# Expert 0's first half on the first 512 tokens, as two parts of 256 tokens, the first started 24 stops earlier in the attention loop

## The chip, the cores and the metric

The kernel runs on one core of a Trainium2 chip. Its engines work side by side, each on its own queue in its own order: TensorE (PE for its matmuls, PEld for its weight loads), VectorE (DVE), ScalarE (ACT), GpSimd (POOL) and SyncE (SP, which issues transfers). The metric is the device time of one execution in microseconds (us); lower is better. Three executions of the kernel before took 1479.65 to 1479.95 us, median 1479.87.

## What is computed

Three layers in a row, all in float32: windowed attention with sink keys, a mixture of 8 experts whose gates come from a Sinkhorn iteration, and a mixture of 8 experts that sends each token to one of them.

```python
# attention: B=2, H=8 heads, S=768 tokens, D=64; 4 sink keys, window 128
scores = where(keep, scale * q @ k.T, -1e9)
a = softmax(scores); x = (a @ v)           # -> 1536 tokens x 512
# first mixture: every expert on every token (w1: 512 x 1024, w2: 1024 x 512)
for e in range(8):
    out += P[:, e:e+1] * (maximum(x @ w1[e], 0) @ w2[e])
# second mixture: the same layer, each token through its best expert alone
```

## The kernel before

**Numbers.** Each float32 operand is split into a high and a low part (tiles that end in h and l). `mm3` (lines 66 to 68) multiplies two such pairs with three matmuls: low weights by high data, high by low, high by high. What a ScalarE copy rounds to the high part, VectorE subtracts from the original to get the low part.

**Attention** goes over 12 blocks of 128 tokens and in each over 4 pairs of heads, 48 pairs in all. It is written as a generator, `attention()`, which runs as a pipeline. In one pass `m` TensorE gets three pieces, with a stop (`yield`) behind each:

- `pv(m - 5)`: attention times V for pair m-5, 18 small matmuls (12 or 6 in the first blocks of a batch) into one PSUM tile, `pv`
- `p_trans(m - 3)`: transposes of the probabilities (`tr`, line 1126), in some passes with a transpose of sink columns (line 1138) or four of the next block's K or Q (line 1003)
- `scores(m)`: 6 matmuls (`sc`)

I call this stretch of TensorE's program **turn j**, j = m-5 from 0 to 47, even and odd by j. An odd turn finishes a group of four heads: ScalarE then copies the `pv` tile to `xh` (line 1172, two instructions) and VectorE subtracts the low part into `xl` (line 994, two instructions). The `pv` tile has one buffer, so the next turn's first matmul waits for `xl`.

**The first mixture is begun inside attention.** Expert 0's first half of the hidden units, which is `unit(0, c)` for a chunk c of 512 tokens, is cut into fill steps of one `mm3`, three matmuls. `l1` (line 178) computes a block of 128 hidden units from four such steps into the PSUM tile `L` and reads it with a ReLU on ScalarE (`hh`, line 192) and a subtraction on VectorE (`hl`, line 193). `l2` (line 195) computes 128 tokens' outputs from four steps into the PSUM tile `y`, which VectorE then copies to `acc` (line 210). For c = 0 and 1 this gives 16 steps of `l1` and 16 of `l2` each; the steps of chunk 2 come behind attention. While attention runs, `L` for these steps has one buffer and `y` has one: the next group's first matmul waits until VectorE has read the last one's.

**What sets the order** is the loop that drives the generator. It counts the stops, n; turn j has the stops n = 3(j+5), 3(j+5)+1 and 3(j+5)+2, behind its three pieces. At n = 63 (turn 16) `unit(0, 0)` is put on the list `fills`, at n = 111 (turn 32) `unit(0, 1)`. At five stops of six (n % 6 < 5) one fill step is put into TensorE's program, except that the stop after a group's fourth step stays empty (`hold`). A unit that has run out also uses up a stop to find that out, and one more for `hold`. What is left of the fills when attention ends is written out in one piece behind it. The order of VectorE, ScalarE and the other queues follows the same sequence.

Two weight tiles are needed: `w1`'s part, split into high and low at n = 12 to 27, and `w2`'s part, split at n = 45 to 60.

Of the kernel before, what the change touches and what calls it, by code (L numbers as in the profile page):

```python
# [8 lines left out]
F32 = mybir.dt.float32  # L9
F32R = mybir.dt.float32r  # L10
I32 = mybir.dt.int32
AF = mybir.ActivationFunctionType
ALU = mybir.AluOpType
# [10 lines left out]
def kernel(  # L24
# [15 lines left out]
    nc = tc.nc  # L40
# [6 lines left out]
    KD = DM // 128  # L47
    CH = 512
    NC = N // CH
    TPC = CH // 128  # L50
# [14 lines left out]
    def mm3(out_ap, ah, al, bh, bl, start, stop):  # L65
        nc.tensor.matmul(out_ap, al, bh, start=start, stop=False)  # L66
        nc.tensor.matmul(out_ap, ah, bl, start=False, stop=False)  # L67
        nc.tensor.matmul(out_ap, ah, bh, start=False, stop=stop)  # L68
# [22 lines left out]
    xh = [xp.tile([128, KD, CH], F32R, name=f"xh{c}") for c in range(NC)]  # L91
    xl = [xp.tile([128, KD, CH], F32R, name=f"xl{c}") for c in range(NC)]
# [56 lines left out]
    def w_load(p, pool):  # L149
        t = pool.tile([128, FB, 512], F32, name="raw", tag="raw")  # L150
        nc.sync.dma_start(t, w_src(p))
        raw_t[p] = t
# [22 lines left out]
    h_t = {}  # L175
    Pm = ctile([128, NT, E], "Pm")

    def l1(g, c, f):
        wh, wl = w_t[2 * g]
        tag = f"L{cnt['l'] % cnt['nl']}"  # L180
        cnt["l"] += 1
        ps = ps_m.tile([128, CH], F32, name="L", tag=tag)
        fs = slice(f * 128, (f + 1) * 128)
        for kk in range(KD):
            mm3(ps, wh[:, kk, fs], wl[:, kk, fs], xh[c][:, kk, :], xl[c][:, kk, :], kk == 0, kk == KD - 1)
            if kk < KD - 1:
                yield None
        s = cnt["h"] % cnt["nh"]
        cnt["h"] += 1
        pool = hp_a if s < 4 else pools["h"]  # L190
        hh, hl = h_t[f] = [pool.tile([128, CH], F32R, name=f"h{x}{s}") for x in "hl"]
        nc.scalar.activation(hh, ps, AF.Relu)  # L192
        nc.vector.scalar_tensor_tensor(hl, ps, 0.0, hh.bitcast(F32), op0=ALU.max, op1=ALU.subtract)  # L193

    def l2(g, c, t):
        wh, wl = w_t[2 * g + 1]
# [18 lines left out]
                nc.vector.tensor_scalar(a, a, Pm[:, blk, 0:1], None, op0=ALU.mult)  # L215
            nc.vector.scalar_tensor_tensor(a, ps, Pm[:, blk, e:e + 1], a, op0=ALU.mult, op1=ALU.add)  # L216

    def unit(g, c):
        for f in range(FB):
            yield from l1(g, c, f)  # L220
            yield f + 1
        for t in range(TPC):
            yield from l2(g, c, t)
            yield FB + t + 1

# [950 lines left out]
    LT, LV = 3, 5  # L1176
# [95 lines left out]
    with tc.manual_schedule():  # L1272
        at = attention()
        fills = []
        hold = False
        for n, _ in enumerate(at):
            if n == 1:
                w_load(0, raw_a)
                load_gates()
            if n in range(12, 32, 5):  # L1280
                if n == 12:
                    split = w_split(0, 4)
                next(split)
            if n == 32:
                w_load(1, raw_a)
            if n in range(45, 65, 5):
                if n == 45:
                    split = w_split(1, 4)
                next(split)
            if n == 100:  # L1290
                prep_gates()
            for c in range(NC - 1):
                if n == 3 * (4 * TPC + LV + 16 * c):
                    fills.append(unit(0, c))
            if fills and n % 6 < 5:
                if hold:
                    hold = False
                else:
                    st = next(fills[0], 0)
                    hold = st is not None  # L1300
                    if st == 0:
                        fills.pop(0)
# [147 lines left out]
```

## Time and profile before

| | us |
|---|---|
| three executions, median | 1479.87 |
| the profiled execution | 1480.35 |
| its span, first to last instruction | 1478.6 |
| TensorE busy with matmuls | 1442.5 |
| VectorE busy | 695.2 |
| ScalarE busy | 455.5 |
| GpSimd busy | 129.8 |

The profiled execution is 0.48 us above the median of the three and lies 1.75 us above its own span. Attention with the fills takes about the first 207 us of the span; the rest is the two mixtures. A busy TensorE in these numbers means that a matmul was in flight; as matmuls overlap, the distance from one start to the next tells more.

### The profile page before, as it was taken

The numbers are of one execution on the slowest core, as the hardware profiler recorded it, in microseconds if no ns is written. First come the engines' busy times: TensorE is split into PE (matmuls) and PEld (weight loads), VectorE is DVE, ScalarE is ACT, GpSimd is POOL, SyncE is SP. The second block draws the span as 40 slices with busy tenths as digits, with TensorE's granted clock in tenths as the row PEclk, the third lists the DMA queues.
The fourth block names the chain that finished last, engine by engine and source line by source line (L and its number), as shares of the span: only waits on it lengthen the run. The fifth ranks groups of instructions, "written<-read, shape, count | busy, mean of one in ns | idle before, by whom it ended". The sixth has DMA issues, their size and how long they took to land. (4 is left out here: it accounts for less than half of the span.)

```text
span 1478.6 us, 18476 instructions
## 1 busy us (share of the span) xinstructions
PE 1442.5 (98%) x7245; PEld 1178.2 (80%) x7245; DVE 695.2 (47%) x1487; ACT 455.5 (31%) x966; POOL 129.8 (9%) x188
## 2 busy tenths in 40 slices
PE   5899999999999999999999999999999999899998
PEld 4777787788888888888888888888888877788886
DVE  5868643553323333332423333242333257877774
ACT  4756532111202211120211112021111133666664
POOL 3634310000000000000000000000000000111111
PEclk9999999999999999999999999999999999999999
DMA  5412102000101010010101000010100041987771
GB/s 110 95 44 59 44 30 86 29 29 29 57 0 58 0 57 29 29 51 7 58 1 57 28 30 31 27 57 1 57 0 0 29 143 44 327 278 263 269 259 56
DMA packets 86029, 105.69 MB, mean 71 GB/s; under 512 B 41518, under 2 KB 41518, under 8 KB 85936
## 3 DMA queue, kind: packets, MB, share of 16 engines
q1 hardware_dynamic: 83056, 96.58, 20.4%
q0 software_dynamic: 2880, 7.87, 1.6%
q8 instruction: 59, 0.97, 0.3%
q14 instruction: 34, 0.28, 0.1%
HBM read 101.29 MB, written 7.86 MB: 74 GB/s over the span
## 5 line engine op out<-in xcount | busy, mean ns | idle before, releaser
L192 ACT ACTIVATE hh<-L 128x512 fp32r<-128x512 f32 x192 | 114.8, 598 | 802.0 <-PE L L68 801.9
L193 DVE SCALAR_TENSOR_TENSOR hl<-L,hh 128x512 fp32r<-128x512 f32 x192 | 132.8, 692 | 355.9 <-ACT hh L192 355.7
L216 DVE SCALAR_TENSOR_TENSOR acc<-y,Pm,acc 128x512 f32<-128x512 f32 x168 | 126.1, 751 | 252.3 <-PE y L68 251.9
L66 PE MATMUL y<-whb,hl 128*128 128x512 f32 x432 | 170.8, 395 | 0.0
L68 PE MATMUL y<-whb,hh 128*128 128x512 f32 x432 | 168.6, 390 | 0.0
L67 PE MATMUL y<-wlb,hh 128*128 128x512 f32 x432 | 168.2, 389 | 0.0
L66 PE MATMUL y<-wha,hl 128*128 128x512 f32 x412 | 163.0, 396 | 0.1
L68 PE MATMUL y<-wha,hh 128*128 128x512 f32 x412 | 160.6, 390 | 0.0
L67 PE MATMUL y<-wla,hh 128*128 128x512 f32 x412 | 160.5, 390 | 0.0
L66 PE MATMUL L<-xh,wla 128*128 128x512 f32 x384 | 152.8, 398 | 0.0
L66 PE MATMUL L<-xh,wlb 128*128 128x512 f32 x384 | 151.0, 393 | 0.0
L68 PE MATMUL L<-xh,wha 128*128 128x512 f32 x384 | 149.7, 390 | 0.0
L68 PE MATMUL L<-xh,whb 128*128 128x512 f32 x384 | 149.6, 390 | 0.0
L67 PE MATMUL L<-xl,wha 128*128 128x512 f32 x384 | 149.6, 390 | 0.0
L67 PE MATMUL L<-xl,whb 128*128 128x512 f32 x384 | 149.6, 390 | 0.0
L68 PEld LDWEIGHTS y<-whb,hh 128*128 128x128 f32 x432 | 81.1, 188 | 17.2
L67 PEld LDWEIGHTS y<-wlb,hh 128*128 128x128 f32 x432 | 81.2, 188 | 16.0
L66 PEld LDWEIGHTS y<-whb,hl 128*128 128x128 f32 x432 | 81.2, 188 | 16.0
L688 POOL DMA_INDIRECT acc<-x2d,ig_s x2 | 2.1, 1051 | 1045.7 <-DVE tmp_d L439 1020.5
L68 PEld LDWEIGHTS y<-wha,hh 128*128 128x128 f32 x412 | 77.4, 188 | 16.1
L66 PEld LDWEIGHTS y<-wha,hl 128*128 128x128 f32 x412 | 77.4, 188 | 15.8 <-DVE acc L210 0.2
L67 PEld LDWEIGHTS y<-wla,hh 128*128 128x128 f32 x412 | 77.5, 188 | 15.0
(313 smaller groups left out, 2358.2 us busy)
## 6 DMA issues: line engine op xcount, KB each, us to landing
raw<-in_moe_w SPq DMA_DIRECT2D x80, 1024.0 KB, 5.5
raw<-in_v SPq DMA_DIRECT2D x12, 256.0 KB, 2.9
raw<-vfb SPq DMA_DIRECT2D x12, 256.0 KB
x2d<-acc SPq DMA_DIRECT2D x12, 256.0 KB, 2.0
raw<-in_k SPq DMA_DIRECT2D x11, 256.0 KB
raw<-in_q SPq DMA_DIRECT2D x11, 256.0 KB, 6.1
raw<-in_k SPq DMA_DIRECT2D x2, 128.0 KB
raw<-in_q SPq DMA_DIRECT2D x2, 128.0 KB
```

Source lines behind the costliest of these rows:

```text
L66: nc.tensor.matmul(out_ap, al, bh, start=start, stop=False)
L67: nc.tensor.matmul(out_ap, ah, bl, start=False, stop=False)
L68: nc.tensor.matmul(out_ap, ah, bh, start=False, stop=stop)
L192: nc.scalar.activation(hh, ps, AF.Relu)
L193: nc.vector.scalar_tensor_tensor(hl, ps, 0.0, hh.bitcast(F32), op0=ALU.max, op1=ALU.subtract)
L216: nc.vector.scalar_tensor_tensor(a, ps, Pm[:, blk, e:e + 1], a, op0=ALU.mult, op1=ALU.add)
L688: nc.gpsimd.indirect_dma_start(out=x, out_offset=None, in_=src, in_offset=bass.IndirectOffsetOnAxis(ap=index(ig_s, ig_d, i), axis=0))
```

## The change

`l1` and `unit` take a range of tokens, and the first fill, `unit(0, 0)`, becomes two units: tokens 0 to 255 put on the list at n = 39 (turn 8), when two blocks are through attention, and tokens 256 to 511 at n = 63. The unit of chunk 1 is still put on the list at n = 111. In the two new units each step of `l1` streams 256 columns instead of 512, so chunk 0 has 32 steps of `l1` at half the width; ReLU and subtraction work on 256 columns, 8 of each instead of 4. The 16 steps of `l2` stay as they are, 8 in each unit.

```diff
-    def l1(g, c, f):
+    def l1(g, c, f, ts=slice(0, CH)):
...
         for kk in range(KD):
-            mm3(ps, wh[:, kk, fs], wl[:, kk, fs], xh[c][:, kk, :], xl[c][:, kk, :], kk == 0, kk == KD - 1)
+            mm3(
+                ps[:, ts], wh[:, kk, fs], wl[:, kk, fs], xh[c][:, kk, ts], xl[c][:, kk, ts], kk == 0, kk == KD - 1
+            )
...
-        nc.scalar.activation(hh, ps, AF.Relu)
-        nc.vector.scalar_tensor_tensor(hl, ps, 0.0, hh.bitcast(F32), op0=ALU.max, op1=ALU.subtract)
+        nc.scalar.activation(hh[:, ts], ps[:, ts], AF.Relu)
+        nc.vector.scalar_tensor_tensor(
+            hl[:, ts], ps[:, ts], 0.0, hh[:, ts].bitcast(F32), op0=ALU.max, op1=ALU.subtract
+        )
...
-    def unit(g, c):
+    def unit(g, c, blks=range(TPC)):
+        ts = slice(blks.start * 128, blks.stop * 128)
         for f in range(FB):
-            yield from l1(g, c, f)
+            yield from l1(g, c, f, ts)
             yield f + 1
-        for t in range(TPC):
+        for t in blks:
...
-            for c in range(NC - 1):
-                if n == 3 * (4 * TPC + LV + 16 * c):
-                    fills.append(unit(0, c))
+            for c, blks in ((0, range(0, 2)), (0, range(2, 4)), (1, range(0, 4))):
+                if n == 3 * (4 * (TPC * c + blks.stop) + LV):
+                    fills.append(unit(0, c, blks))
```

By the program's order the places of the fills change as follows. Before, unit (0, 0) runs from turn 16 to 31 and unit (0, 1) from turn 33, with its last 4 steps behind turn 47. After, the first part runs from turn 8 to 19, the second from turn 21 to 32 and unit (0, 1) from the end of turn 33, with its last 4 steps behind turn 47 and one more step between turn 47's products and them.

TensorE, turn 8, from the last of its 18 products on (`tr` and `L1` are the transposes, `sc` the scores, `L` the fill). Before:

```order
L68 MATMUL pv_129<-skh_1099,vsh_959 64x128
L1126 MATMUL tr_1206<-ident_69,P_1048 128x128 x4
L1138 MATMUL L1_1214<-ident_69,pk_1087 64x128
L66 MATMUL sc_1221<-kh_576,ql_1041 128x272
L67 MATMUL sc_1221<-kl_577,qh_1040 128x272
```

After:

```order
L68 MATMUL pv_129<-skh_1099,vsh_959 64x128
L66 MATMUL L_1206<-xh0_95,wla0_736 128x256
L67 MATMUL L_1206<-xl0_98,wha0_735 128x256
L68 MATMUL L_1206<-xh0_95,wha0_735 128x256
L1131 MATMUL tr_1210<-ident_69,P_1048 128x128 x4
L1143 MATMUL L1_1218<-ident_69,pk_1087 64x128
L66 MATMUL L_1206<-xh0_95,wla0_736 128x256
L67 MATMUL L_1206<-xl0_98,wha0_735 128x256
L68 MATMUL L_1206<-xh0_95,wha0_735 128x256
L66 MATMUL sc_1228<-kh_576,ql_1041 128x272
```

Two steps of 256 columns stand in a turn that had none; the same holds for turns 9 to 15.

TensorE, turn 43, from the end of its products to the start of turn 44's (`y` is the fill's output; another number is another group of four steps in the same buffer). Before:

```order
L68 MATMUL pv_129<-skh_3244,vsh_2418 64x128
L66 MATMUL y_3418<-wha1_1324,hl0_2827 128x512
L67 MATMUL y_3418<-wla1_1325,hh0_2826 128x512
L68 MATMUL y_3418<-wha1_1324,hh0_2826 128x512
L1126 MATMUL tr_3422<-ident_69,P_3247 128x128 x4
L66 MATMUL y_3418<-wha1_1324,hl1_2967 128x512
L67 MATMUL y_3418<-wla1_1325,hh1_2966 128x512
L68 MATMUL y_3418<-wha1_1324,hh1_2966 128x512
```

After:

```order
L68 MATMUL pv_129<-skh_3302,vsh_2476 64x128
L66 MATMUL y_3385<-wha1_1341,hl3_3357 128x512
L67 MATMUL y_3385<-wla1_1342,hh3_3356 128x512
L68 MATMUL y_3385<-wha1_1341,hh3_3356 128x512
L1131 MATMUL tr_3486<-ident_69,P_3308 128x128 x4
L66 MATMUL y_3495<-wha1_1341,hl0_2962 128x512
L67 MATMUL y_3495<-wla1_1342,hh0_2961 128x512
L68 MATMUL y_3495<-wha1_1341,hh0_2961 128x512
```

Before, turn 43 held the first steps of one group; now it holds the fourth step of a group and, behind four transposes, the first of the next.

VectorE at the same place, from turn 43's reciprocal on (`xl` is the attention output's low part, `COPY` the emptying of `y`, the rest low parts of transposes). Before:

```order
L1109 RECIPROCAL rs_3411<-rs_3411 128x2
L994 TENSOR_TENSOR xl2_100<-pv_129,xh2_97 64x2x128 x2
L994 TENSOR_TENSOR acc8_3428<-tr_3422,pt0_3427 128x512
L210 COPY acc5_82<-y_3418 128x512
L994 TENSOR_TENSOR acc9_3465<-tr_3459,pt1_3464 128x512
```

After:

```order
L1114 RECIPROCAL rs_3475<-rs_3475 128x2
L999 TENSOR_TENSOR xl2_100<-pv_129,xh2_97 64x2x128 x2
L214 COPY acc4_81<-y_3385 128x512
L999 TENSOR_TENSOR acc8_3492<-tr_3486,pt0_3491 128x512
L999 TENSOR_TENSOR acc9_3526<-tr_3520,pt1_3525 128x512
```

The copy that empties `y` moved from the even turn 44 to directly behind the odd turn's `xl`. In turns 45 and 47 it now stands behind `xl` in the same way.

## Rows read from the trace of the kernel before

**Rows 1.** The page: busy us, share of the span, instructions of each engine.

```profile
PE 1442.5 (98%) x7245; PEld 1178.2 (80%) x7245; DVE 695.2 (47%) x1487; ACT 455.5 (31%) x966; POOL 129.8 (9%) x188
```

**Rows 2.** Waits of TensorE from 51.4 to 207.4 us: total, times, longest.

```profile
PE pv L66 <- DVE xl L994: 1.7, 6, 0.5
```

**Rows 3.** Stretches: length, PE, PEld, DVE, ACT, POOL busy (count), PEclk, DMA share, GB/s.

```profile
28.00:32.00 4.00, 2.69 (x24) 2.08 (x21) 3.22 (x18) 3.11 (x10) 2.44 (x5) 1.00 0.45 104
32.00:36.00 4.00, 3.64 (x26) 3.12 (x27) 3.52 (x15) 3.17 (x10) 2.58 (x4) 0.61 0.14 30
64.41:70.91 6.50, 6.28 (x62) 5.03 (x62) 5.08 (x19) 5.23 (x17) 5.11 (x7) 1.00 0.39 83
77.36:86.41 9.05, 9.05 (x73) 7.00 (x74) 5.79 (x19) 5.32 (x16) 5.41 (x7) 1.00 0.27 59
95.42:112.69 17.27, 17.27 (x143) 13.42 (x141) 10.91 (x38) 9.48 (x30) 4.66 (x9) 1.00 0.23 52
112.69:118.83 6.14, 5.97 (x46) 4.48 (x45) 5.00 (x19) 4.12 (x14) 3.39 (x8) 1.00 0.36 78
118.83:125.46 6.63, 6.54 (x48) 4.95 (x48) 5.63 (x20) 4.35 (x13) 2.56 (x4) 1.00 0.16 36
125.46:133.13 7.67, 7.17 (x62) 5.64 (x61) 6.88 (x23) 4.52 (x14) 4.02 (x6) 1.00 0.38 83
133.13:141.14 8.01, 7.34 (x61) 5.67 (x61) 7.29 (x23) 4.85 (x15) 3.58 (x6) 1.00 0.10 24
141.14:207.39 66.25, 66.10 (x527) 51.95 (x526) 38.53 (x125) 32.03 (x92) 23.20 (x42) 1.00 0.15 37
```

**Rows 4.** PE in time, turns 13 and 14: start us, us, instruction [idle before].

```profile
67.36 0.27 PE L66 MATMUL pv<-pt,vl 128*64 128x128 f32 x1
...
70.91 0.24 PE L66 MATMUL pv<-acc,vl 128*64 128x128 f32 x1 [0.22 <-DVE xl L994]
```

**Rows 5.** PE in time, turn 20: one fill step and the transposes behind it.

```profile
97.06 0.50 PE L66 MATMUL L<-xh,wla 128*128 128x512 f32 x1
97.39 0.40 PE L67 MATMUL L<-xl,wha 128*128 128x512 f32 x1
97.63 0.39 PE L68 MATMUL L<-xh,wha 128*128 128x512 f32 x1
97.86 0.60 PE L1126 MATMUL tr<-ident,P 128*128 128x128 f32 x4
```

**Rows 6.** PE in time, turn 26: scores with 256 columns.

```profile
121.72 0.28 PE L67 MATMUL sc<-kl,qh 64*128 64x256 f32 x2
121.84 0.28 PE L68 MATMUL sc<-kh,qh 64*128 64x256 f32 x2
```

**Rows 7.** All engines in time, turn 43 (odd): products, a fill step, transposes, xh, xl.

```profile
189.09 0.28 PE L66 MATMUL pv<-pt,vl 128*64 128x128 f32 x1
...
190.73 0.50 PE L66 MATMUL y<-wha,hl 128*128 128x512 f32 x1
...
190.84 0.77 ACT L1172 ACTIVATE xh<-pv 64x256 fp32r<-64x256 f32 x2
...
191.53 0.60 PE L1126 MATMUL tr<-ident,P 128*128 128x128 f32 x4
191.64 0.85 DVE L994 TENSOR_TENSOR xl<-pv,xh 64x256 fp32r<-64x256 f32 x2
...
191.89 0.47 PE L66 MATMUL y<-wha,hl 128*128 128x512 f32 x1
```

**Rows 8.** All engines in time, turns 25 and 26: y emptied, next group's first matmul.

```profile
118.72 0.69 DVE L210 COPY acc<-y 128x512 f32<-128x512 f32 x1
...
119.46 0.50 PE L66 MATMUL y<-wha,hl 128*128 128x512 f32 x1
```

**Rows 9.** PE, then DVE in time, turn 47: the first fill step behind it, xl.

```profile
204.52 0.50 PE L66 MATMUL y<-wha,hl 128*128 128x512 f32 x1
...
205.42 0.85 DVE L994 TENSOR_TENSOR xl<-pv,xh 64x256 fp32r<-64x256 f32 x2 [1.60 <-ACT xh L1172]
```

**Rows 10.** DVE groups by form, 0 to 222 us: count, busy, mean ns, idle before.

```profile
L193 DVE SCALAR_TENSOR_TENSOR hl<-L,hh 128x512 fp32r<-128x512 f32 x12 | 8.3, 692 | 19.2 <-ACT hh L192 19.2
```

## The prediction

> **What bounds the kernel now.** The page first: TensorE is busy for 98% of the span [rows 1], so the question is not which engine bounds but where TensorE loses time inside attention, since behind it nothing of the change is left. The view of waits from the first moved step (51.4 us) to the end of the fills (207.4 us) shows one wait that counts: an even turn's first product waits for `xl`, 1.7 us in 6 times [rows 2]. Everything else in those 156 us is TensorE's own work, one matmul behind the other. So a step that is moved pays only what idle time it covers; its matmuls cost the same elsewhere.
>
> **How much idle time there is to cover.** Turns 8 to 15 hold no step. A pair of them takes 6.50 us, a pair with four full steps 9.05 us [rows 3]. So a full step costs 2.55/4 = 0.64 us in place, though its three matmuls need 0.33 + 0.24 + 0.23 = 0.80 us from start to start [rows 5]. The difference is idle time that the step covers: at the turn from odd to even, 0.22 us or a little more per pair [rows 4], and at changes of shape between products, transposes and scores.
>
> **A half-width step.** The trace has no fill matmul with 256 columns. The nearest row, scores with 256 columns, has 0.12 us from one to the next [rows 6]; a full-width matmul has 0.235 us [rows 5]. I take 0.12 us, half the full one, and 0.115 us less for the first, so 0.22 + 0.12 + 0.12 = 0.46 us for the step, 0.34 us less than a full one: 0.64 - 0.34 = 0.30 us in place. From below no gain is left to find, since half the columns cannot take less than half of 0.80 us. From above: the weight load could come out of its cover. Four transposes with weights of 128 columns start 0.11 us apart (0.60 us for four, less the 0.27 us that a last one lasts, over three) [rows 5], and that is the most that a load adds to each.
>
> The Trainium skill ("TensorE: Matmul & The Clock Gate", The mechanism) says that a weight load overlaps with matmuls in flight only when the row groups differ. Here all fill matmuls use the same 128 rows, and still a full-width one follows the last after 0.235 us, where 0.21 us would be the columns alone at the page's 2.4 GHz (an estimate) and the load would come on top; so the trace speaks against it for full width. For half width no row here shows it. By that rule the sum would be that of the second rival.
>
> **The sum by stretches**, each against the profiled execution:
>
> - Turns 8 to 15: 16 half steps come in, 16 x 0.30 = **+4.8**. This price has the covered waits in it.
> - Turns 16 to 19: eight full steps before, eight after: 0.
> - Turns 20 to 23: eight full steps leave, seven half steps come: -8 x 0.64 + 7 x 0.30 = **-3.0**.
> - Turns 24 to 31 (28.45 us in four pairs [rows 3]): 16 full steps leave, nine half and seven full come, -3.0 at these prices. But here VectorE is busy for 5.00 + 5.63 + 6.88 + 7.29 = 24.8 of 28.45 us [rows 3]. Its own fill work falls from five instructions of 0.69 us [rows 10] to one of these and three of about 0.42 us (half of the 0.85 us for two `xl` of 256 columns [rows 7]), 1.5 us less. If it keeps all of its 3.65 us of idle time, the stretch loses 1.5 us and no more. I take **-2.0**, nearer to VectorE's bound, because its waits there are chains through ScalarE that a shorter TensorE turn does not shorten.
> - Turn 32 to the end of the fills (66.25 us [rows 3]): one more full step, +0.64, less what it covers in turn 32: **+0.3** (0 to 0.7).
>
> So far +0.1 us: the steps are paid for, the idle time is covered, and TensorE is met by VectorE further on. What decides is the next term.
>
> **New waits in the last unit.** The extra unit costs one more empty pass through the list, so unit (0, 1) starts at n = 116 instead of 114. Its groups of four then end in odd turns instead of even ones. This is the price of the shift, and nothing of it is in the diff. VectorE works in order, and in an odd turn the two `xl` stand ahead of the reading of `y` or `L`. In turn 43 the products begin at 189.09 us, `xh` runs 190.84 to 191.61, `xl` 191.64 to 192.49 [rows 7]. Behind that now stands the copy of `y`, 0.69 us, so to 193.18; a next group's first matmul starts 0.05 us behind the copy's end (118.72 + 0.69 = 119.41, matmul 119.46) [rows 8], so 193.23. TensorE gets there behind the four transposes, at 191.89 [rows 7]: it waits 1.3 us. Turn 45 is the same, 1.3 us. In turn 47 the fourth step begins at 204.52 us and lasts 0.80; `xl` ends at 206.27 [rows 9], the copy at 206.96, and the next step stands right behind: 207.01 - 205.32 = 1.7 us. Queued behind each waiting matmul is TensorE's whole program, turns 44 to 47 and then chunk 2, and no later stretch up to 207 us has idle time of TensorE that could give it back. Together **+4.3**.
>
> `L` is hit the same way in turns 35, 37 and 39. There the reading ends 3.40 us (`xl`'s end, 192.49 - 189.09 [rows 7]) + 0.69 [rows 10] + 0.05 = 4.14 us behind the turn's start. TensorE comes to the next step behind the scores: turn 13 without a step takes 70.91 - 67.36 = 3.55 us with a wait of 0.22 [rows 4], so 3.3, and with the fourth step (0.64 to 0.80) about 4.0 us. It waits 0.15 us, twice; in turn 39, which has no K or Q transposes (about 0.45 us), 0.6 us. **+0.9**. Both bounds for these waits: 3 us if VectorE gets to its queue earlier than in turn 43, 6.5 us if ScalarE's copies are pushed back by the ReLUs.
>
> Sum: 4.8 - 3.0 - 2.0 + 0.3 + 4.3 + 0.9 = **+5.3 us**. The profiled execution, 1480.35 us, would become 1485.65; it lies 0.48 us above the median, 1479.87, so I forecast **1485.2 us**.
>
> Taken at nothing: four more pairs of ReLU and subtraction at half width, on ScalarE and VectorE, which in turns 8 to 15 have a pair's 6.50 us with 5.23 and 5.08 us of work [rows 3] and get 1.2 us more per pair with the steps (0.4 us each per pair if that cover were gone). No transfer is moved past another: the loads of weights, K, Q and V keep their stops. `w2`'s split is still ahead of the first step that reads it; the fourth piece is needed only by the group's fourth step, in turn 17.
>
> **The rivals.**
>
> 1. *No waits in the tail.* The reading of `y` and `L` ends before TensorE is there, because `xh` and `xl` come earlier relative to the products than in turn 43. Then +5.3 - 5.2 = +0.1, and with turns 24 to 31 at -3.0 it is -0.9: **1479.0 to 1480.0 us**, not slower. It decides from about 2.9 us of tail waits downwards, where 0.1 + 2.9 is the 3 us that can be told. For it: VectorE is busy less than half the time over the program [rows 1]. Against it: in the odd turn its `xl` cannot start before ScalarE has read the products, and that row is measured. Chance 0.11; faster by more than 0.2% would need turns 24 to 31 to take TensorE's own time alone, 0.02 of it.
> 2. *Weight loads without cover at half width*: 48 added matmuls at up to 0.11 us, +5.2 on top of the forecast, **1490.4 us**. Against it: the transposes, with half the columns again, already run at the pace of the load alone. Chance 0.04.
> 3. *The clock falls in the thinner stretch or in the tail.* Behind four us with 2.69 us of busy TensorE the granted clock was 0.61 of full speed in the next four, mostly the 1.2 GHz level [rows 3]. One such fall costs 0.39 x 4 = 1.6 us: **1486.8 us**. For it: three new stalls over a microsecond each. Against it: the steps around them are dense, and turns 8 to 15 with their waits keep 1.00 [rows 3]. Chance 0.08.
>
> **The chances.** The forecast has 0.77, its own range is 1483 to 1488 (turns 24 to 31 from -3.0 to -1.5, tail waits 3 to 6.5). Behind it stand rival 3 with 0.08, rival 1 with 0.11, rival 2 with 0.04. The range of 8 in 10 reaches a little to both sides, 1482.5 to 1488.5; rival 1 and rival 2 stay out. A measurement here tells a change from none at about 0.2%, these 3 us. Slower by more than that (above 1482.8): forecast, rivals 2 and 3, less the forecast's lowest part, 0.86. Within 0.2%: 0.12. Faster: 0.02.
>
> **What the changed kernel's profile would show.** Right: turns 8 to 15 at about 7.7 us a pair; half-width matmuls 0.12 us apart; in the waits of TensorE a new line, `y` released by the copy of `acc`, three times and over 1.2 us each in the last 15 us of the fills, and `L` by `hl`; fewer waits for `xl` in turns 9 to 15. Wrong: no wait at the copies (then rival 1), half-width matmuls 0.2 us apart (rival 2), a stretch with a granted clock under 1 behind 51 us (rival 3), or turns 24 to 31 over 28 us, where I would have the wrong bound for VectorE.

## The result

The changed kernel takes **1488.88 us** (median of 6 runs, 1487.34 to 1490.53), the kernel before 1479.91 us (median of 6, 1479.65 to 1480.13): a ratio of 1.0060, 95% interval 1.0049 to 1.0071, or 9.0 us more. The forecast was 1485.2 us with a range of 1482.5 to 1488.5. The sign was right, and so was most of the sum, but the time lies 0.4 us above the range. The profiled execution of the changed kernel took 1490.53 us (span 1488.8), that of before 1480.35 (span 1478.6); between these two lie 10.2 us, and they are taken apart here.

The page of the changed kernel, its line of busy times, against [rows 1]: TensorE works 4.9 us more, and the span is 10.2 us longer.

```profile
PE 1447.4 (97%) x7293; PEld 1183.9 (80%) x7293; DVE 694.9 (47%) x1491; ACT 455.4 (31%) x970; POOL 129.8 (9%) x188
```

TensorE's waits from 51 to 216 us, the stretch of [rows 2] (what waited, what released it: us in total, times, longest):

```profile
PE y L66 <- DVE acc L214: 3.8, 3, 1.6
PE pv L66 <- DVE xl L999: 0.9, 3, 0.4
PE L L66 <- DVE hl L195: 0.6, 1, 0.6
PE L L1143 <- DVE rs L1113: 0.5, 1, 0.5
...
```

The first row is the forecast's new line: `y`, released by the copy to `acc`, three times. The third is the wait for `L` in turn 39 (those of turns 35 and 37, under 0.2 us each, are too short for a row). The fourth was not forecast: a sink transpose (L1143, the transpose of the sink columns) waits. Waits for `xl` have halved.

Two stretches of before that [rows 3] does not have (turns 8 to 15; all that follows the fills), then six of the changed kernel: turns 8 to 15, 20 to 23, 24 to 31, turn 32 to the end of the fills, and the two stretches at half clock. Columns as in [rows 3], the granted clock is the third number from the end.

```profile
51.46:77.36 25.90, 24.94 (x244) 19.94 (x245) 20.90 (x75) 20.56 (x60) 16.88 (x22) 1.00 0.29 64
...
207.39:1478.60 1271.21, 1258.12 (x5758) 1033.65 (x5756) 555.72 (x1002) 337.38 (x620) 38.50 (x38) 1.00 0.21 73
```

```profile
51.24:83.08 31.84, 31.23 (x292) 26.04 (x292) 21.98 (x78) 21.82 (x64) 17.35 (x22) 1.00 0.24 52
...
101.12:115.49 14.37, 14.37 (x140) 12.19 (x139) 10.78 (x41) 8.51 (x28) 4.45 (x9) 1.00 0.27 60
115.49:141.63 26.14, 25.03 (x215) 20.00 (x214) 23.29 (x84) 18.58 (x57) 14.41 (x22) 1.00 0.27 61
141.63:215.46 73.83, 69.23 (x529) 53.68 (x528) 38.55 (x123) 31.98 (x92) 22.51 (x42) 0.98 0.15 44
211.37:214.78 3.41, 3.41 (x10) 2.67 (x9) 0.00 (x0) 0.00 (x0) 0.00 (x0) 0.50 0.51 196
215.46:1488.80 1273.34, 1259.43 (x5758) 1034.38 (x5756) 555.48 (x1002) 337.34 (x620) 38.48 (x38) 1.00 0.21 72
1283.15:1286.57 3.42, 3.42 (x11) 2.65 (x10) 1.89 (x3) 2.34 (x5) 0.00 (x0) 0.50 1.04 384
```

Held against the forecast's terms (each stretch from the first product of a turn to that of another; e1, e2 and e9 are experiments below):

| stretch | before | forecast | after | difference | e1 | e2 | e9 |
|---|---|---|---|---|---|---|---|
| up to turn 8 | 51.46 | 0 | 51.24 | -0.2 | 51.94 | 50.90 | 51.54 |
| turns 8 to 15 | 25.90 | +4.8 | 31.84 | +5.9 | 32.27 | 25.90 | 31.04 |
| turns 16 to 19 | 18.06 | 0 | 18.04 | 0.0 | 18.04 | 18.03 | 18.03 |
| turns 20 to 23 | 17.27 | -3.0 | 14.37 | -2.9 | 14.35 | 17.27 | 14.37 |
| turns 24 to 31 | 28.45 | -2.0 | 26.14 | -2.3 | 26.15 | 28.47 | 26.13 |
| turn 32 to the fills' end | 66.25 | +5.5 | 73.83 | +7.6 | 66.64 | 71.84 | 66.65 |
| behind the fills | 1271.2 | 0 | 1273.3 | +2.1 | 1272.3 | 1271.3 | 1272.5 |

So three terms are off: turns 8 to 15 by 1.1 us, the tail (turn 32 to the end of the fills) by 2.1, and 2.1 us come in the second mixture, of which the change moves nothing.

**The tail in time.** Turn 43 of the changed kernel, VectorE and the TensorE row that waits for it (start us, us, instruction, [idle before <- releaser]):

```profile
192.80 0.85 DVE L999 TENSOR_TENSOR xl<-pv,xh 64x256 fp32r<-64x256 f32 x2
...
193.68 0.69 DVE L214 COPY acc<-y 128x512 f32<-128x512 f32 x1
...
194.43 0.50 PE L66 MATMUL y<-wha,hl 128*128 128x512 f32 x1 [1.13 <-DVE acc L214]
```

It is the chain of the forecast: the two `xl`, behind them the copy, 0.05 us behind that the matmul. From the transposes' start to this matmul it takes 1.73 us, where turn 44, without a wait, has 0.44 us to the next instruction: 1.29 us lost, 1.3 were forecast (the view's 1.13 counts from the modelled end of the transposes). Turn 45 loses the same 1.29. In turn 47 the next group starts at 211.01 us, 1.72 us behind its turn (209.06 + 0.23); 1.7 were forecast. Right behind that wait TensorE runs at half clock:

```profile
211.01 0.52 PE L66 MATMUL y<-wha,hl 128*128 128x512 f32 x1 [1.57 <-DVE acc L214]
211.35 0.60 PE L67 MATMUL y<-wla,hh 128*128 128x512 f32 x1
211.75 0.63 PE L68 MATMUL y<-wha,hh 128*128 128x512 f32 x1
```

The matmuls from 211.35 on are 0.40 to 0.43 us apart and not 0.235. From turn 47's first fill step to the end of the fills it takes 6.97 us; the same 15 matmuls with the same wait took 5.42 us at full clock (e2, below). The fall costs **1.55 us** here.

### The profile page after: what moved, and what is told of

Its sections match the earlier page's. It is cut to its first block, busy times and chain, and to the rows that moved or that the text cites. A ratio compares the mean times of both kernels' runs of the same rounds, so it can differ in the third digit from the quotient of the medians.

```text
span 1488.8 us, 18576 instructions
## 1 busy us (share of the span) xinstructions
PE 1447.4 (97%) x7293; PEld 1183.9 (80%) x7293; DVE 694.9 (47%) x1491; ACT 455.4 (31%) x970; POOL 129.8 (9%) x188
## 5 line engine op out<-in xcount | busy, mean ns | idle before, releaser
L194 ACT ACTIVATE hh<-L 128x512 fp32r<-128x512 f32 (+1 forms) x196 | 115.4, 589 | 801.5 <-PE L L68 801.0
L195 DVE SCALAR_TENSOR_TENSOR hl<-L,hh 128x512 fp32r<-128x512 f32 (+1 forms) x196 | 133.3, 680 | 348.7 <-ACT hh L194 348.4
L66 PE MATMUL L<-xh,wla 128*128 128x512 f32 (+1 forms) x400 | 156.8, 392 | 0.8 <-DVE hl L195 0.6
L68 PE MATMUL L<-xh,wha 128*128 128x512 f32 (+1 forms) x400 | 152.3, 381 | 0.0
L67 PE MATMUL L<-xl,wha 128*128 128x512 f32 (+1 forms) x400 | 152.2, 381 | 0.0
```

The costliest lines, as they stand in the source:

```text
L194: nc.scalar.activation(hh[:, ts], ps[:, ts], AF.Relu)
L195: nc.vector.scalar_tensor_tensor(hl[:, ts], ps[:, ts], 0.0, hh[:, ts].bitcast(F32), op0=ALU.max, op1=ALU.subtract)
```

## The experiments

Theory: the loss is the shift by two stops (the waits for `y` and `L`, with a fall of the clock behind them) plus a wait in turns 8 to 15. Rivals: the loss is in the early, half-wide steps themselves, or in something that no stall of the tail explains. All kernels of one group ran on one chip with the kernel before; its median was 1480.33 us beside e1 to e4, 1480.07 beside e5 to e8, 1480.23 beside e9 to e11.

**e1: the last unit begins at stop 114 again.**

```
                     st = next(fills[0], 0)
+                    if st == 0 and n > 100 and len(fills) > 1:
+                        fills.pop(0)
+                        st = next(fills[0])
```

> The changed kernel, but the unit of expert 0's first half on the second 512 tokens takes its first step at the stop at which the second part is found exhausted, so that it begins at stop 114, as it did before the change, and not at 116; each of its groups then has its fourth step in an even turn again. All else is the changed kernel. Theory A (the shift by two stops costs the waits for `y` in turns 43, 45 and 47 and for `L` in turns 35, 37 and 39, 5.2 us in the changed kernel's trace, and the stalls bring the fall of the granted clock at 211 us, 1.7 us more): 1488.9 - 5.2 - 1.7 = 1482.0 us, within 1481.0 to 1483.0, with no half-speed stretch between 200 and 220 us. Rival B (the waits go, the clock's fall has another cause): 1483.7 us, with the half-speed stretch still there. Rival C (the tail is not where the time is lost; the loss is in the early part and in the second mixture): 1488 us or more.

Measured: 1482.97 us (1481.08 to 1484.50), ratio 1.0015 (1.0006 to 1.0025). That is 5.9 us less than the changed kernel. Two stretches of its trace:

```profile
142.75:209.39 66.64, 66.64 (x529) 52.43 (x528) 38.35 (x123) 31.92 (x92) 22.54 (x42) 1.00 0.15 37
200.00:220.00 20.00, 20.00 (x111) 16.45 (x112) 7.17 (x16) 4.42 (x9) 0.53 (x5) 1.00 0.18 53
```

TensorE is busy all the way from turn 32 to the end of the fills, the clock holds 1.00, and of 7.6 us only 0.4 remain. Theory A, at the upper end of its range, 1.0 us above the value that it gave. Two thirds of the change's loss hang on a two-stop shift.

**e2: before the change, with the last unit two stops late.** Nothing else is touched.

```
-            if fills and n % 6 < 5:
+            if fills and n % 6 < 5 and n not in (114, 115):
```

> The kernel before the change, with one edit: the stops 114 and 115 are skipped, so that the second unit begins at 116 as in the changed kernel. Nothing is half as wide and nothing starts early. Theory A (the phase of that unit alone makes the waits and the clock's fall): 1479.9 + 5.5 + 1.7 = 1487.1 us, within 1485.0 to 1487.5, with PE waiting about 1.3 us for the copy of `y` in turns 43 and 45 and 1.6 in turn 47. Rival B (the waits come, the fall of the clock doesn't): 1485.4 us. Rival C (the waits need what the early parts do to the engines' order): 1480 us.

Measured: 1485.64 us (1485.23 to 1487.00), ratio 1.0036 (1.0022 to 1.0050), 5.3 us more than before. Its waits of TensorE for `y`, and its tail:

```profile
PE y L66 <- DVE acc L210: 3.8, 3, 1.6
```

```profile
140.57:212.41 71.84, 67.14 (x527) 52.08 (x526) 38.69 (x125) 32.10 (x92) 23.15 (x42) 1.00 0.16 45
200.00:220.00 20.00, 17.30 (x98) 13.70 (x97) 6.19 (x13) 2.55 (x5) 0.53 (x5) 1.00 0.15 53
```

The same three waits, to a hundredth: the tail takes 5.6 us more, 0.3 of it beyond the waits themselves (5.3). But the clock stays at 1.00. That is rival B: the same stalls do not always bring the fall.

**e3: the copy of `y` on ScalarE.**

```
         if g == 0:
-            nc.vector.tensor_copy(a, ps)
+            if c == 1:
+                nc.scalar.activation(a, ps, AF.Copy)
+            else:
+                nc.vector.tensor_copy(a, ps)
```

> The changed kernel, with one edit: for the second 512 tokens of expert 0's first half the copy of `y` to its accumulator is done on ACT in place of DVE, where it no longer stands behind the two `xl` subtractions of an odd turn. The unit still begins at stop 116. Theory A (each `y` wait is the time that the copy stands in DVE's row behind `xl`, and these waits bring the clock's fall): the waits of turns 43, 45 and 47, 4.2 us together, go, the fall at 211 us goes, the waits for `L` (1.0 us) stay: 1488.9 - 4.2 - 1.7 = 1483.0 us, within 1482 to 1484. Rival B (the waits go, the fall stays): 1484.7 us. Rival C (ACT is as late as DVE there, behind `xh` and `pt`): 1488 to 1489 us.

Measured: 1485.22 us (1484.90 to 1486.41), ratio 1.0036 (1.0024 to 1.0047), 3.7 us less than the changed kernel. The waits for `y`, and in turn 43 ScalarE and the last matmul of the group that fills `y`:

```profile
PE y L66 <- ACT acc L215: 1.2, 3, 0.7
```

```profile
192.13 0.77 ACT L1180 ACTIVATE xh<-pv 64x256 fp32r<-64x256 f32 x2
192.60 0.40 PE L68 MATMUL y<-wha,hh 128*128 128x512 f32 x1
193.03 0.60 ACT L215 ACTIVATE acc<-y 128x512 f32<-128x512 f32 x1
```

The waits fall from 3.8 to 1.2 us by this view, not to nothing. ScalarE's two `xh` do not hold the copy up: they end at 192.90 us, the group's last matmul ends at 193.00, and the copy starts 0.03 us behind that (0.04 and 0.03 in turns 45 and 47). So what is left is the copy itself, 0.60 us between a group's last matmul and the next group's first, with only four transposes between the two, in turn 47 with nothing. A free queue does not remove that part of the phase's price. There is no half-speed stretch in the tail, which takes 69.62 us in place of 73.83: 4.2 us less, 1.55 of them the fall's. Theory A in kind (VectorE's row was the wait, the fall went with it), its time 2.2 us above the forecast.

**e4: e1, and the split of `w2` moved away from the Relu.**

```
-            if n in range(45, 65, 5):
+            if n in (45, 50, 53, 58):
```

> The kernel of e1 (unit of the second 512 tokens begins at stop 114), and besides the second weight's split is done at the stops 45, 50, 53 and 58 in place of 45, 50, 55 and 60, so that ACT's copy for the split no longer stands right ahead of the Relu at stop 55. To be held against e1, on the same chip. Theory A (in the changed kernel the transposes of turn 14 wait 0.65 us longer than in turn 8 because DVE's subtraction after the Relu stands behind ACT's split copy, and the `L1` buffer comes free late): e1 less 0.5 us, within 0.2 to 0.9, with the piece of turn 14 between its first transpose and the next step down from 1.08 us to under 0.7. Rival B (the subtraction on DVE alone delays that buffer, whatever ACT does): no difference to e1, or the same wait in another even turn.

Measured: 1482.36 us (1481.59 to 1483.22) against 1482.97 of e1, which the spread of the runs does not tell apart. In the traces the sink transpose of turn 14 waits 0.48 us in e1 and 0.17 in e4:

```profile
79.06 0.27 PE L1143 MATMUL L<-ident,pk 128*64 128x128 f32 x1 [0.48 <-DVE rs L1113]
```

```profile
78.63 0.27 PE L1143 MATMUL L<-ident,pk 128*64 128x128 f32 x1 [0.17 <-DVE rs L1113]
```

From turn 14's first transpose to its sink transpose it takes 0.77 us where e1 takes 1.08, not under 0.7; turns 10 and 12 keep their 0.57 and 0.71 us. ScalarE's copy for the split is a part of turn 14's wait and no more; e9 finds the rest.

**e5: the changed kernel again, unchanged**, for a second profiled execution.

> The changed kernel once more, unchanged, for a second profiled execution. Open is whether the half-speed stretches at 211 us and at 1283 us belong to the kernel or to one execution: the kernel of e2 had the same stalls of PE in turns 43, 45 and 47, to within 0.01 us each, and no half-speed stretch between 200 and 220 us. Theory A (the falls differ from execution to execution; those behind the stalls come in some only): the stretch from the start of turn 32 to the second 512 tokens' end is either 73.8 us with a fall or 72.1 without, and the times spread over 3 us again, 1487 to 1490.5. Rival B (with the early parts ahead the fall always comes): 73.8 us again, the half-speed stretch there again, the median at 1489 us.

Measured: 1490.59 us (1488.05 to 1491.36), ratio 1.0064 (1.0047 to 1.0080). Its tail and its two half-speed stretches:

```profile
141.91:215.75 73.84, 69.26 (x529) 53.68 (x528) 38.56 (x123) 31.97 (x92) 22.49 (x42) 0.98 0.15 44
211.72:215.13 3.41, 3.41 (x10) 2.63 (x9) 0.00 (x0) 0.00 (x0) 0.00 (x0) 0.50 0.55 214
1283.51:1286.92 3.41, 3.41 (x10) 2.65 (x9) 1.89 (x3) 2.67 (x6) 0.16 (x1) 0.50 1.03 380
```

Both falls are there again, behind the same waits. But both profiled executions (1490.53 and 1490.62 us) lie in the upper half of this kernel's ten runs: five are at 1490.5 or above, the others at 1487.3 to 1489.0. So that every run has both falls is not shown, and the spread speaks against it.

**e6: all fill steps one stop later, no stops lost between units**, so that each group ends behind the scores of an odd turn.

```
-            if fills and n % 6 < 5:
+            if fills and n % 6 < 5 and n != 39:
...
                     st = next(fills[0], 0)
+                    if st == 0 and len(fills) > 1:
+                        fills.pop(0)
+                        st = next(fills[0])
```

> The changed kernel with its fill steps one stop later, the first at stop 40, and each unit following the last without a lost stop, so that every group of four has its fourth step behind the scores of an odd turn, from the first part on; there DVE has the subtraction for `ql` behind it when the Relu's subtraction is queued. The last unit begins at stop 112. Theory A (in turns 10, 12 and 14 PE waits 1.08 us for the `L1` buffer, which DVE's `ql` holds because the Relu's subtraction stands ahead of it; and the tail's waits are of the phase): the pieces of turns 10, 12 and 14 from the transposes to the next step are back at 0.43 to 0.50 us, turns 8 to 15 take 30.8 us and not 31.8, the tail has no waits for `y` and `L`: 1488.9 - 1.1 - 5.2 = 1482.6 less what the falls of the clock had, 1481 to 1482.5. Rival B (the buffer comes late for another reason, GpSimd's row): turns 8 to 15 still take 31.8 us and the time is that of e1, 1483 us.

Measured: 1488.34 us (1486.31 to 1490.02), ratio 1.0056 (1.0040 to 1.0073). Neither theory: the tail is clean (the third stretch below, 66.28 us at clock 1.00), turns 8 to 15 win only 0.4 us, and turns 24 to 31 take 31.85 us in place of 26.14. Turns 8 to 15, 24 to 31 and the tail, then TensorE's two largest waits from 51 to 214 us (all but 0.3 us of them in turns 24 to 31):

```profile
50.98:82.45 31.47, 31.18 (x292) 26.24 (x293) 22.95 (x79) 21.57 (x63) 17.91 (x22) 1.00 0.24 53
115.12:146.97 31.85, 26.95 (x216) 21.12 (x215) 23.62 (x84) 18.51 (x57) 14.70 (x23) 0.95 0.27 60
146.97:213.25 66.28, 66.28 (x527) 51.34 (x525) 38.49 (x123) 31.93 (x92) 22.29 (x40) 1.00 0.11 29
```

```profile
PE L L66 <- DVE hl L195: 2.8, 3, 1.3
PE y L66 <- DVE acc L214: 1.3, 1, 1.3
```

These turns have 6 or 12 products in place of 18. What is late there is the next group's first step: it waits up to 1.3 us for a Relu's subtraction or for a copy that now stands behind the last turn's scores, and behind the last of these stalls the clock falls once more (0.95 in the stretch). The phase that is right for the tail is wrong for the thin turns; there is no one phase for the whole list.

**e7: halves in place.** Before the change, with 8 of the first unit's 16 steps issued as two times three matmuls of 256 columns.

```
+            if (g, c) == (0, 0) and kk in (1, 2):
+                for ts in (slice(0, 256), slice(256, 512)):
+                    mm3(ps[:, ts], ..., xh[c][:, kk, ts], xl[c][:, kk, ts], False, False)
+            else:
                 mm3(ps, wh[:, kk, fs], ...
```

> The kernel before the change, with one edit: in expert 0's first half on the first 512 tokens the second and third of the four steps of each group are issued as two times three matmuls of 256 columns in place of three of 512, at the same stop; nothing starts early, the number of steps is the same. So 8 of 16 steps are in halves. Theory A (width itself costs nothing: half-width matmuls follow each other at 0.12 us as whole ones at 0.235, and the dearer half step, 0.46 us in place of half of 0.80, is the change from one kind of work to another, paid per step): each halved step stays within 0.05 us of 0.80, the time within 0.5 us of before. Rival B (at half width the weight loads of 0.19 us set the pace): 6 x 0.19 = 1.14 us a step, 8 x 0.34 = 2.7 us more, 1483 us.

Measured: 1481.01 us (1479.83 to 1482.56), ratio 1.0004 (0.9994 to 1.0013): no difference that can be told, though the median is 0.9 us above that of before on this chip, more than the 0.5 that theory A allowed. Turn 17 in time, the first and the last matmul of a halved step and what follows it, and the stretch of turns 20 to 23, 17.27 us in [rows 3]:

```profile
84.55 0.38 PE L66 MATMUL L<-xh,wla 128*128 128x256 f32 x1
...
85.25 0.29 PE L68 MATMUL L<-xh,wha 128*128 128x256 f32 x1
85.38 0.49 PE L1133 MATMUL tr<-ident,P 128*128 128x128 f32 x3
```

```profile
96.66:113.97 17.31, 17.31 (x155) 14.37 (x153) 10.92 (x38) 9.48 (x30) 4.68 (x9) 1.00 0.22 50
```

Six half-width matmuls take 0.83 us here (0.81 to 0.83 in the four steps that stand ahead of transposes), three full ones 0.80, and from turn 16 on no stretch is more than 0.05 us longer than before up to the end of the fills: theory A. Width by itself costs next to nothing. What makes two half steps (2 x 0.46 us) dearer than a full one (0.80) is the extra 0.1 us that the first matmul behind another kind of work takes, once per step.

**e8: e6 with the split of `w2` at stops 45, 49, 55 and 60.**

```
-            if n in range(45, 65, 5):
+            if n in (45, 49, 55, 60):
```

> The kernel of e6, and the second weight's split at the stops 45, 49, 55 and 60, so that none of its copies on ACT stands right ahead of a Relu. To be held against e6 on the same chip. Theory A (behind the scores the Relu's subtraction holds no one up, whatever ACT does): no difference to e6 beyond 0.3 us. Rival B (the split's copies still hold up the Relu and through it PE): 0.3 to 0.9 us less than e6.

Measured: 1488.88 us (1486.70 to 1489.39) against 1488.34 of e6. In the trace turn 12's first fill step comes 0.18 us behind its sink transpose and not 0.56 (rival B, in that place), but the time does not show it.

**e9: e1 with `ql` ahead of the Relu.** At a first part's fourth steps the waiting subtractions are issued before the fill step.

```
+                    if n % 6 == 1 and n < 63:
+                        flush()
                     st = next(fills[0], 0)
```

> The kernel of e1 (last unit at stop 114) with one edit: at the stop in which a group of the first part has its fourth step, the subtractions that wait in `later` (for `pt` and for `ql`) are issued before the fill step and not after the scores, so that on DVE `ql` stands ahead of the Relu's subtraction. To be held against e1 (1482.97 us, turns 10, 12 and 14 with 0.56, 0.71 and 1.08 us from the first transpose to the sink transpose). Theory A (the `L1` buffer that the sink transpose waits for is held by `ql`, which stood behind the Relu's subtraction): those three pieces are back at 0.43 to 0.50 us, turns 8 to 15 take 30.8 us where the clock doesn't fall in them, 1.1 us less than e1: 1481.9 us. Rival B (it is GpSimd's row or the order on ACT that is late): the pieces stay, 1483 us.

Measured: 1480.99 us (1480.22 to 1482.03), ratio 1.0002 (0.9993 to 1.0012), 2.0 us less than e1, which ran on another chip. VectorE in turns 13 and 14, first in the changed kernel (the last row is TensorE's sink transpose), then in e9:

```profile
75.44 0.42 DVE L195 SCALAR_TENSOR_TENSOR hl<-L,hh 128x256 fp32r<-128x256 f32 x1 [1.32 <-ACT hh L194]
...
76.50 0.69 DVE L999 TENSOR_TENSOR acc<-tr,pt 128x512 fp32r<-128x512 f32 x1
...
77.11 0.68 DVE L999 TENSOR_TENSOR ql<-L,qh 128x512 fp32r<-128x512 f32 x1
...
77.93 0.27 PE L1143 MATMUL L<-ident,pk 128*64 128x128 f32 x1 [0.49 <-DVE rs L1113]
```

```profile
74.88 0.68 DVE L999 TENSOR_TENSOR ql<-L,qh 128x512 fp32r<-128x512 f32 x1
75.55 0.42 DVE L195 SCALAR_TENSOR_TENSOR hl<-L,hh 128x256 fp32r<-128x256 f32 x1
```

`ql` is the low part of the next block's Q, which VectorE subtracts out of the PSUM buffer `L1`. In the changed kernel VectorE stands 1.32 us waiting for the Relu on ScalarE, and `ql` ends at 77.79 us; the sink transpose, which needs that buffer, starts at 77.93. In e9 `ql` has ended at 75.56 us. Turns 10, 12 and 14 are back at 0.43 to 0.44 us each (0.57, 0.72 and 1.08 in the changed kernel), and turns 8 to 15 take 31.04 us, of which the end of a half-speed stretch in turn 8 has 0.25. Theory A. Of the 1.23 us that these turns are shorter than in e1, about 0.2 are e1's longer half-speed stretch there; the other 0.8 us by which the medians differ are not explained. The view of waits had named another instruction (`rs`, which ended at 77.86), since it names the last thing that ended. That it is `ql` the traces tell: the sink transpose starts 0.14 us behind the end of `ql` here and in e4, 0.15 in e1, and 0.14 in a turn of e11 where no `rs` stands between them.

**e10: e2 with the copy of `y` done twice**, which makes each of the three stalls longer by one copy. By its edit (`1 + c`) the third 512 tokens, behind the fills, get three copies each; there TensorE waits for none of them.

```
-            nc.vector.tensor_copy(a, ps)
+            for _ in range(1 + c):
+                nc.vector.tensor_copy(a, ps)
```

> The kernel of e2 (before the change, last unit at stop 116) with one edit: the copy of `y` of the second 512 tokens is issued twice on DVE, so that each of the waits for `y` in turns 43, 45 and 47 is longer by one copy, 0.6 to 0.7 us. Open is whether longer stalls of PE there bring the half-speed stretch that both profiled executions of the changed kernel have behind them and e2's has not. Theory A (a longer idle stretch of PE does it): waits of 2.0 us, a half-speed stretch between 200 and 220 us, 1485.6 + 2.1 + 1.5 = 1489.2 us. Rival B (the length of the stalls doesn't decide): the waits are longer, no half-speed stretch there, 1487.7 us.

Measured: 1493.13 us (1492.05 to 1493.25), ratio 1.0082 (1.0066 to 1.0097), 7.5 us more than e2. The stalled matmul of turn 43, and the two stretches at half clock:

```profile
193.79 0.50 PE L66 MATMUL y<-wha,hl 128*128 128x512 f32 x1 [1.85 <-DVE acc L211]
```

```profile
203.47:210.30 6.83, 6.83 (x33) 5.30 (x31) 0.28 (x1) 0.00 (x0) 0.00 (x0) 0.50 0.00 0
213.71:220.02 6.31, 5.28 (x12) 4.13 (x13) 0.94 (x2) 0.00 (x0) 0.00 (x0) 0.50 0.37 142
```

Theory A, and more than its number: with stalls of 1.85, 1.84 and 2.29 us in place of 1.13, 1.13 and 1.57 by this view there are two half-speed stretches where e2's execution had none. From turn 32 to the end of the fills it takes 79.34 us against 71.84; three copies more are 2.2 us of these 7.5, and the other 5.3 are put down to the clock. All four runs lie within 1.2 us, so the loss is not one execution's.

**e11: double steps.** Six half-width matmuls per step for the two parts, so half as many steps; the first part from stop 51, the last unit from 114.

```
-            if kk < KD - 1:
+            if kk < KD - 1 and (ts == slice(0, CH) or kk % 2 == 1):
...
+            for n0, c, blks in ((51, 0, range(0, 2)), (63, 0, range(2, 4)), (112, 1, range(0, 4))):
+                if n == n0:
```

> The changed kernel with half as many steps for the two parts: a step of theirs is six matmuls of 256 columns (two of the four slices of the sum) and not three; the first part starts at stop 51, the second follows it without a lost stop, stop 92 is skipped, and the last unit begins at stop 114 with its groups' fourth steps in even turns. So the change of one kind of work to another, about 0.1 us each time, is paid for 16 steps and not 32, and no Relu comes right ahead of `ql`. Theory A (the change's loss is those extra switches, the waits for `L1` and the phase; without them the early start fills what PE waits there are): 1478.0 to 1480.0 us, not slower than before. Rival B (the thinner turns 24 to 29 or DVE give new waits): 1481 to 1484 us.

Measured: 1485.10 us (1484.10 to 1485.68), ratio 1.0029 (1.0018 to 1.0040). Theory A misses; rival B in kind, and 1.1 us above its range too. Turns 24 to 31 in its trace, and the three largest waits of TensorE from 50 to 145 us:

```profile
116.39:144.20 27.81, 23.09 (x204) 18.18 (x202) 23.20 (x80) 18.10 (x55) 13.60 (x21) 1.00 0.25 55
```

```profile
PE pv L66 <- DVE xl L999: 2.3, 5, 0.8
PE L L1143 <- DVE ql L999: 1.4, 1, 1.4
PE L L66 <- DVE hl L195: 1.2, 2, 1.0
```

It has 10 fill steps in turns 24 to 31 where the kernel before has 16, which is 3.8 us less at 0.64 us each, and the stretch is only 0.6 us shorter than before (28.45 us [rows 3]), with TensorE idle for 4.7 us: here it waits 1.8 us for `xl`, 1.4 for `ql` and 1.0 for a Relu's subtraction. It is not the amount of VectorE's work that does it: the changed kernel has the same there (23.29 us against 23.20), holds 16 steps, nine of them half as wide, and takes 26.14 us. Which order in the queues does it was not tested. Nor are the double steps cheaper early on: turns 8 to 15 take 30.95 us with seven of them, 5.05 more than before, and turns 20 to 23 give back 0.6 us in place of 2.9.

No version measured beats the kernel before. Of those that start early e9 comes nearest; its time can't be told from that of before.

## Why the prediction was right, and where it failed

**In short.** The waits of the tail, which the forecast called decisive, came as forecast. What its sum lacked are a cost that it took at nothing (ReLU and subtraction in turns 8 to 15, 1.1 us), a rival that it left out with a chance of 0.08 (the clock's fall, 1.55 us), and the stretch behind the fills, where it said that "nothing of the change is left" (2.1 us, cause open).

**Right: the mechanism that decides.** The waits for `y` came at 1.29, 1.29 and 1.72 us where 1.3, 1.3 and 1.7 were forecast, in the turns named; those for `L` at 0.19, 0.18 and 0.62 us where 0.15, 0.15 and 0.6 were forecast. Together 5.3 us against 5.2. By e3 the copy's own length, with no queue ahead of it, is a part of this; the forecast's chain holds both. e2 shows them in the old kernel with the shift alone, e1 shows them gone from the new one without it. The range for them (3 to 6.5 us) was wider than the rows of turn 43 needed.

**Right: the price of a half step.** 0.46 us from start to start, as put together from scores of 256 columns. Turns 20 to 23 gave back 2.9 us (forecast 3.0). Turns 8 to 15 of e9, less the clock's 0.25, cost 4.9 us more than before (forecast 4.8). Rival 2 falls: in e7 halved steps cost 0.01 to 0.03 us more. The Trainium skill ("TensorE: Matmul & The Clock Gate", The mechanism) has a weight load overlap with matmuls in flight only where the row groups differ; a sentence ahead of that also lets loads into a background weight buffer go ahead of matmuls in flight. This trace does not agree with the "only": half-width matmuls that all use the same 128 rows follow each other after 0.12 us, each with a weight load of 0.19 us; whether the background buffer does it no run here shows. A load in e9, whose matmul starts at 80.44 us and the next at 80.56:

```profile
80.32 0.19 PEld L67 LDWEIGHTS L<-xl,wha 128*128 128x128 f32 x1
```

**Near in number, but not for its reason: turns 24 to 31.** They gave back 2.3 us, between the bounds of 1.5 and 3.0; 2.0 were taken because VectorE was to keep most of its idle time. Its work fell as forecast, by 1.5 us (24.80 to 23.29), but its idle time did not stay: 3.65 us before, 2.85 after. TensorE's idle time fell as well, from 1.43 to 1.11 us. So that VectorE held the other 0.7 us back is not shown.

**Failed, first: "taken at nothing".** The four more pairs of Relu and subtraction were put at nothing in turns 8 to 15, since VectorE and ScalarE have idle time there. They do, but the pair comes at a stop where `ql` is not yet issued, so VectorE waits for the Relu with `ql` behind it, and the `L1` buffer comes free late: 0.14, 0.29 and 0.65 us in turns 10, 12 and 14, 1.1 us. e9 shows it. The forecast asked of each added wait of the tail what is queued behind it, and did not ask it here. The kernel before had a hint: the view behind [rows 2] has more rows than the one shown there, the next of which is

```profile
PE L L1138 <- DVE ql L994: 0.7, 1, 0.7
```

A sink transpose (turn 30) already waits for `ql`, so the one wait that "counts" was not the only one, and not everything else was TensorE's own work.

**Failed, second: the clock.** Rival 3 had a chance of 0.08 with "three new stalls over a microsecond each" for it. Both profiled executions of the changed kernel have the fall behind the stalls; its price, 1.6 us, was right (1.55). It deserved a far larger chance than 0.08. What spoke against it ("the steps around them are dense") did not decide: e10 with the longer stalls has two falls, e2 with the same stalls as the changed kernel has none. No trace here has a fall in the tail without the stalls (none in e1, e4, e6 and e9, where they are gone, nor in e3, where they are shorter), and e6 and e8 have one in turns 24 to 31, where e6 stalls three times for 1.3 us; e11 stalls there up to 1.4 us and has none. So stalls go before the fall, but do not bring it each time; why e2's execution escaped stays open.

**Failed, third: the rest of the program** was put at nothing. In both profiled executions of the changed kernel TensorE's wait for a gather (a transfer that fetches the tokens of an expert by index) in the second mixture is longer, and a half-speed stretch stands behind it. The first row is of the changed kernel, the second of before:

```profile
1282.64 0.63 PE L702 MATMUL xst<-ident,acc 128*128 128x128 f32 x4 [2.42 <-DMA acc<-x2d,ig_d]
```

```profile
1273.67 0.63 PE L697 MATMUL xst<-ident,acc 128*128 128x128 f32 x4 [1.56 <-DMA acc<-x2d,ig_d]
```

Of the 2.1 us the later gather has 0.9; the half clock is left with some 1.2. No instruction differs there, and a wait as long as the changed kernel's (2.48 us) stands in e9 too, so it does not hang on the tail's stalls. Of the other traces e5, e8 and e11 have the half-speed stretch at this place too (1273.1, 1272.8 and 1273.2 us behind the fills), e1, e3 and e4 have one at a wait 15 us earlier (1272.0 to 1272.3), e2, e7 and e9 one 25 us earlier (1271.3, 1271.7 and 1272.5; e8 has one there as well), e6 and e10 none (1271.2 and 1271.4). So up to 2 us hang on whether and where the clock falls there and on the gather. What decides that, and what delays the gather, stays open; with it stays open how much of the 9.0 us is the change's own doing: by the medians e1 keeps 2.6 us over before and e2 5.3, together 7.9.

With the three in it the sum is 5.3 + 1.1 + 1.55 + 2.1 = 10.1 us, against 10.2 between the profiled executions. That it closes to 0.1 us is in part luck: the tail has 0.5 us more than the forecast's terms and the clock give, and turns 24 to 31 and the time up to turn 8 have 0.3 and 0.2 less than forecast.

## What to carry to other kernels

A list of work that is dealt out by a modulo has a phase: before anything in it is lengthened, work out at which stop each later unit now begins, and what stands on the in-order engines ahead of the instruction that frees its buffer; here a shift by two stops cost more than all the rest of the change. An added instruction on an engine with idle time is free only if nothing that the bounding engine needs is queued behind its wait. And repeated stalls of TensorE like those of the tail are to be priced twice, for the waits and for the half clock that may follow.

## What the runs showed of the hardware that was not expected

- The granted clock fell to the 1.2 GHz level behind stalls of TensorE in turns 43, 45 and 47: waits of 1.1, 1.1 and 1.6 us by the waits' view, with TensorE at work between them, gave a half-speed stretch of 3.4 us in two profiled executions out of two; the same waits in e2 gave none; in e10 waits of 1.85, 1.84 and 2.29 us gave 13 us at half speed.
- Whether and where the clock falls is not the same in kernels that are alike up to that point: up to turn 8 no kernel here differs from another, and the traces have from none (e2) to two half-speed stretches there, with turn 8 starting between 50.6 and 52.3 us.
- A weight load that is recorded at 0.19 us did not set the pace of matmuls of 256 columns: each with a load of its own, they follow each other after 0.12 us, those of 512 columns after 0.235.
